# Small tables of eight pair tiles loaded by SyncE, and the last pair's additions split differently

## The chip, the cores and the metric

The kernel runs on one core of a Trainium2 chip. The metric is the device time of one execution in microseconds (us); the median of several executions is compared. The engines are called TensorE (PE, matrix products), VectorE (DVE), ScalarE (ACT), GpSimd (POOL) and SyncE (SP, which here only starts transfers). All of them run at the same time and wait for each other by semaphores.

## What is computed

The first half is a gated linear attention over 4 batches, 8 heads, 768 steps and a head size of 48. Its output, turned into 3072 tokens of 384 values, goes through a router that picks 2 of 8 experts for each token, and then through the experts, each a two-layer network of 384 to 1024 to 384.

```python
for t in range(S):
    state = alpha[:, :, t, :, None] * state + np.einsum('bhd,bhe->bhde', k[:, :, t], v[:, :, t])
    y[:, :, t] = np.einsum('bhd,bhde->bhe', q[:, :, t], state)
...
logits = x @ w_gate
noise_scale = np.log1p(np.exp(x @ w_noise))
noisy_logits = logits + noise_scale * noise
top2 = np.argpartition(-noisy_logits, 2, axis=1)[:, :2]
...
for e in range(E):
    for k in range(2):
        mask = top2[:, k] == e
        h = np.maximum(x[mask] @ w1[e], 0.0)
        out[mask] += top2_w[mask, k, None] * (h @ w2[e])
```

## The kernel before

The attention runs in 24 chunks of 128 tokens. While it does, the router enters each token twice in a table in device memory: one list per expert, each entry four words (token, gate, other expert, rank in the other expert's list). The entries are written by 48 scatters of GpSimd.

The experts then run in 24 *pairs*: a pair is two tiles of 128 tokens of one expert. The pairs 0 to 7 are the first 256 entries of each of the eight experts; the pairs 8 to 23 are two more pairs for each expert, the experts in falling order. Where a pair starts in its list is fixed for the pairs 0 to 13 (`PLANNED`), and for the later ones it is read from a small plan that VectorE computes from the counts. Three smaller tiles (two of 32 tokens, one of 64) take what is left over of the lists; they are worked on beside the pairs 13 to 22. Anything beyond would run under a condition at the end, which isn't met here.

Each pair goes through these steps:

- `load_tab` (lines 1066 to 1076) loads the pair's table, 256 entries of 16 bytes, into a tile `tab` of 128 partitions x 2 x 8. Tiles of that name rotate through six buffers, so that a load waits for the last reader of the table six pairs earlier. It also waits for the scatters that write the entries. SyncE loads it with one transfer for the pairs 0, 1 and 5 to 8; GpSimd loads the others, the pairs 2 to 4 with one transfer and from pair 9 on with two of 128 entries each. From pair 14 on the first row is read from the plan into a register of the engine that loads.
- `load_w1` and `load_w2` (lines 1078 to 1090) load an expert's two matrices on SyncE, where the expert changes. There are two buffers for each.
- `find_rows` on VectorE computes from `tab` which rows to fetch; `gather` on GpSimd fetches the tokens (`x_in`), and `turn_x` transposes them on TensorE.
- 11 products of the first layer and 7 of the second follow, which TensorE sums up in the PSUM banks named a, b, c and A, B, C (`product1`, line 1180, and `product2`, line 1187). The matrices and tokens are added and subtracted beforehand (`sum_w1`, `sum_w2`, `sum_x`), which saves one product in eight in each layer.
- `summed` (line 1199) computes gate x bank + a second term into the tile `o`. `get_prev` (line 921) gathers what the output holds for the pair's tokens into `prev`, and waits for every earlier scatter into the output. `combine` (line 1208) computes previous x second + o, where second is 1 for the second of a token's experts and 0 for the first; `put_pair` scatters the rows to the output (line 929).

The order is written out by hand: each step has a nominal time, pair i is at 20 i, all steps are sorted by that number, and each engine gets its instructions in the sorted order and runs them strictly in it, as soon as their waits are over. `load_tab` is at 20 i - 32, `load_w1` at 20 i - 29.5, `load_w2` at 20 i - 19.8, `find_rows` at 20 i - 27; the first 32-token tile starts loading its table (GpSimd) and its weights (SyncE, by a register that is read from the plan) at 232, the next at 312.

For the last pair, pair 23, `combine` and `put_pair` are replaced by `combine_last` and `put_last`. There the bank C becomes the left half (columns 0 to 191) of the first tile, and the bank A, whose last product ends last, the left half of the second tile.

Of the kernel before, what the change touches and what calls it, by code (L numbers as in the profile page):

```python
# [13 lines left out]
ALU = mybir.AluOpType  # L14
# [4 lines left out]
def kernel(  # L19
# [32 lines left out]
    nc = tc.nc  # L52
    B, H, S, D = q.shape
    N, DM = out.shape
    E, _, F = moe_w1.shape
    C = 128
# [871 lines left out]
    def put_tile(rows, at, beside=()):  # L928
        put = nc.gpsimd.indirect_dma_start(out=out, out_offset=bass.IndirectOffsetOnAxis(ap=at, axis=0), in_=rows,  # L929
                                           in_offset=None, bounds_check=N - 1, oob_is_err=False)  # L930
        for earlier in order["puts"] + order["gets"]:
            tc.declare_no_dep(put.ins, earlier, reason="different rows, or one that this tile has read")
        order["puts"].append(put.ins)
# [6 lines left out]
    def of_plan(i, what, most, engine=mybir.EngineType.SP):  # L940
        return nc.values_load(plan[0:1, i, what:what + 1], engines=[engine], min_val=0, max_val=most,
                              skip_runtime_bounds_check_because=WHY)
# [93 lines left out]
    HF, HD = F // 2, DM // 2  # L1036
# [7 lines left out]
    def pairs(on):  # L1044
# [12 lines left out]
        n_ = block([C, HD], "n", 3)  # L1057
        o = one.tile([C, 2, DM], F32, name="o")
        tabs, wheres, weights, bank = {}, {}, {}, {}
# [5 lines left out]

        def load_tab(i):

            by, engine = (nc.sync, mybir.EngineType.SP) if i < 2 or 5 <= i <= E else (nc.gpsimd, mybir.EngineType.Pool)
            row = order_of[i] * RMAX + [0, R2, 2 * R2][rounds[i]] if i < PLANNED else of_plan(FIRST_PAIR + i - E, 1, TROWS - R2, engine)
            tabs[i] = on["tab"].tile([C, 2, 8], F32, name="tab")  # L1070
            parts = 1 if i <= E else 2
            for s in range(parts):
                take_tile(by.dma_start(out=tabs[i][:, ds(s, 2 // parts), 0:4],
                                       in_=table.bitcast(F32)[ds(row + s * C, R2 // parts), :].rearrange("(s p) w -> p s w", p=C)),
                          2 if i < E else NU)
# [50 lines left out]
        def plus(to, p, q):  # L1126
            nc.vector.tensor_tensor(to, p, q, op=ALU.add)  # L1127
# [65 lines left out]
        gate = lambda i, s: tabs[i][:, s, 1:2]  # L1193

        def scaled(i, to, src, s):
            nc.scalar.activation(to, src, AF.Copy, scale=gate(i, s))  # L1196

        def summed(i, s, d, name, to_add):
            nc.vector.scalar_tensor_tensor(o[:, s, ds(d * HD, HD)], bank[name], gate(i, s), to_add, op0=ALU.mult, op1=ALU.add)

        def get_prev(i):
            for s in range(2):
                get_rows(prev[i % 2][:, s], wheres[i][:, s, 1:2])
# [6 lines left out]
        def combine_last(i):  # L1210

            rows, second = prev[i % 2], tabs[i][:, :, 6:7]
            nc.vector.scalar_tensor_tensor(rows[:, 0], rows[:, 0], second[:, 0], o[:, 0], op0=ALU.mult, op1=ALU.add)
            nc.vector.scalar_tensor_tensor(rows[:, 1, HD:DM], rows[:, 1, HD:DM], second[:, 1], o[:, 1, HD:DM],
                                           op0=ALU.mult, op1=ALU.add)
            nc.vector.tensor_scalar(out=rows[:, 1, 0:HD], in0=rows[:, 1, 0:HD], scalar1=second[:, 1], scalar2=None,
                                    op0=ALU.mult)

        def put_last(i):
            rows = prev[i % 2]  # L1220
            put_tile(rows[:, 0], wheres[i][:, 0, 0:1])
            nc.vector.scalar_tensor_tensor(rows[:, 1, 0:HD], bank["A"], gate(i, 1), rows[:, 1, 0:HD], op0=ALU.mult, op1=ALU.add)
            put_tile(rows[:, 1], wheres[i][:, 1, 0:1])

        def put_pair(i):
            for s in range(2):
# [7 lines left out]
        def steps(i):  # L1234
            w = lambda f, a: w1_(i, f, a)
            v = lambda f, d: w2_(i, f, d)
            late = 11.0 if i >= E and divmod(i - E, 2) in [(g, 0) for g in AFTER_GROUP] else 0.0
            after = 3.5 if i > E and divmod(i - E, 2) in [(g, 1) for g in AFTER_GROUP] else 0.0
            early = {0: EARLY_0, 1: EARLY_1, E: {"find": T * E - 21.5, "gather": T * E - 21.0}}.get(i, {})
            at = lambda name, t: early.get(name, T * i + t) - T * i  # L1240
            return [(T * i + t, go) for t, go in (
                (at("tab", -32.0), lambda: load_tab(i)), (at("w1", -29.5), lambda: load_w1(i)), (at("w2", -19.8), lambda: load_w2(i)),
                (at("find", -27.0), lambda: find_rows(i)), (at("gather", -26.0), lambda: gather(i)),
                (at("turn", -10.1), lambda: turn_x(i)), (at("sum_x", -7.9), lambda: sum_x(i)),
                (at("s0", -16.5), lambda: sum_w1(i, 0)), (at("s1", -15.8), lambda: sum_w1(i, 1)), (at("s3", -7.5), lambda: sum_w1(i, 3)),
                (at("s2", -7.4), lambda: sum_w1(i, 2)),
                (at("t0", -5.2), lambda: sum_w2(i, 0)), (at("t1", -2.5), lambda: sum_w2(i, 1)), (at("t2", 0.1), lambda: sum_w2(i, 2)),
                (at("t3", 4.4), lambda: sum_w2(i, 3)),
                (0.0, lambda: product1("a", w(0, 0), x(0, 0), True)),
                (0.9, lambda: product1("c", w(0, 1), x(1, 0), True)),  # L1250
                (0.95, lambda: nc.scalar.copy(m[0], bank["a"])),
                (1.8, lambda: product1("c", w(0, 2), x(2, 0))),
                (2.7, lambda: product1("b", ws[0], xs[0], True)),
                (2.75, lambda: plus(hs[0][0], bank["c"], m[0])),
                (3.6, lambda: product1("a", ws[1], xs[1])),
                (3.65, lambda: nc.scalar.copy(m[1], bank["b"])),
                (4.5, lambda: product1("b", ws[3], x(1, 1))),
                (4.55, lambda: nc.scalar.copy(m[2], bank["a"])),
                (4.6, lambda: relu(hs[0][0])),
                (5.4, lambda: product1("a", ws[2], xs[2])),  # L1260
                (6.3, lambda: product1("a", w(1, 2), x(2, 1))),
                (7.2, lambda: product1("b", w(0, 2), x(2, 1))),
                (7.25, lambda: plus(hs[1][1], bank["a"], m[1])),
                (8.0, lambda: relu(hs[1][1])),
                (8.1, lambda: product1("a", w(1, 1), xs[3])),
                (8.15, lambda: plus(hs[0][1], bank["b"], m[2])),
                (8.9, lambda: relu(hs[0][1])),
                (9.0, lambda: product1("a", w(1, 2), xs[4])),
                (9.5, lambda: plus(hx[0], hs[0][1], hs[1][1])),
                (9.6, lambda: less(hx[1], hx[0], hs[0][0])),  # L1270
                (9.95, lambda: relu(hs[1][0], bank["a"])),
                (10.0, lambda: less(hx[3], hs[1][0], hx[1])),
                (10.1, lambda: less(hx[2], hs[0][0], hs[0][1])),
                (10.55, lambda: product2("A", hs[0][0], v(0, 0), True)),
                (11.9, lambda: product2("B", hx[0], wt[0], True)),
                (11.95, lambda: scaled(i, n_[0], bank["A"], 0)),
                (13.2, lambda: product2("A", hx[1], wt[1])),
                (13.25, lambda: scaled(i, n_[1], bank["B"], 1)),
                (14.6, lambda: product2("B", hx[3], v(1, 1))),
                (14.65, lambda: scaled(i, n_[2], bank["A"], 0)),  # L1280
                (15.9, lambda: product2("A", hx[2], wt[2])),
                (15.95, lambda: summed(i, 0, 1, "B", n_[2])),
                (17.3, lambda: product2("C", hs[1][0], v(1, 0), True)),
                (17.35, lambda: summed(i, 1, 1, "A", n_[1])),
                (18.6, lambda: product2("A", hs[1][1], wt[3])),
                (18.65, lambda: summed(i, 0, 0, "C", n_[0])),
                (8.5 + late + after, lambda: get_prev(i))) + (((20.0 - 0.05, lambda: scaled(i, o[:, 1, 0:HD], bank["A"], 1)),
                (20.9 + late / 2.4, lambda: combine(i)),
                (22.2 + late / 2.4, lambda: put_pair(i))) if i < NPAIR - 1 else
                ((19.2, lambda: combine_last(i)), (20.0, lambda: put_last(i))))]  # L1290

        return steps, clear_rows, T

# [241 lines left out]
```

## Time and profile before

| | us |
|---|---|
| median of 3 runs | 670.87 |
| lowest and highest run | 669.77, 671.29 |
| the profiled execution, its whole time | 673.52 |
| its span, first to last instruction | 671.9 |
| TensorE busy (matmuls) | 653.7 |
| VectorE busy | 459.2 |
| GpSimd busy | 315.0 |
| ScalarE busy | 270.9 |
| transfers started by GpSimd | 237 |

The profile numbers times from the start of the span. The attention takes the time to about 169, where pair 0 begins. Each pair's first product starts, in us, at 189.1 (pair 1), 209.0, 229.3, 249.4, 269.4, 289.7, 309.8, 329.8 (8), 349.9 (9), 369.8, 389.7, 409.6, 429.5, 451.7, 473.3, 493.2 (16), 513.1, 535.3, 556.8, 576.8, 596.7, 620.4 and 643.2 (23). The busy times and durations come from the one profiled execution.

A line of a timeline has the start, the duration, the engine, the source line, the operation, the tile written `<-` the tiles read, their shapes, and how many such instructions are merged; in brackets, how long the engine had been idle and who released it. The list of waits has the waiting line, who it waited for, and the sum of the waits, their number and the longest. Both can be asked for one engine and one stretch. A second table view gives the busy time of each engine in several stretches.

### The profile page before, as it was taken

The page shows a single profiled execution, that of the slowest core. Times are in us where ns is not written, and L with a number is a line of the kernel's source. Part 1 is how long each engine was busy: PE and PEld are TensorE (multiplying, and loading weights), DVE is VectorE, ACT ScalarE, POOL GpSimd, SP SyncE. Part 2 cuts the span into 40 slices and gives each one's busy share as a digit, 9 for nine tenths or more (in the row PEclk, how much of TensorE's full clock was granted, in tenths as well). Part 3 has the DMA queues.
Part 4 walks back from the last instruction along what each step waited for, and adds up shares of the span by engine and source line. Part 5 has one row for each costly group of instructions (what it writes and reads, how often), then busy time and mean ns, then how long its engine had stood idle before and what let it go on. Part 6 is the DMA issues. An engine that isn't in the chain of part 4 may idle for free. (4 is left out here: it accounts for less than half of the span.)

```text
span 671.9 us, 14849 instructions
## 1 busy us (share of the span) xinstructions
PE 653.7 (97%) x5605; PEld 626.8 (93%) x5605; DVE 459.2 (68%) x1081; ACT 270.9 (40%) x582; POOL 315.0 (47%) x420
## 2 busy tenths in 40 slices
PE   8899999999999999999999999999999999999994
PEld 6898998998999999999999999999999999998894
DVE  6678888885878888767577666575564765647432
ACT  3667667564443434332323332333323333233330
POOL 5362585684344575775514335422654225540231
PEclk9999999999999999999999999999999999999998
DMA  9999988977556657677203476148362483620121
GB/s 140 149 202 173 215 136 155 221 146 218 197 171 231 232 144 231 160 226 255 73 26 129 133 260 215 56 137 293 103 209 67 146 283 113 214 70 8 47 65 37
DMA packets 144181, 105.63 MB, mean 157 GB/s; under 512 B 109255, under 2 KB 131410, under 8 KB 144100
## 3 DMA queue, kind: packets, MB, share of 16 engines
q1 hardware_dynamic: 131716, 80.37, 45.8%
q0 software_dynamic: 12240, 23.80, 11.7%
q8 instruction: 47, 0.77, 0.5%
q10 hardware_dynamic: 144, 0.41, 0.2%
q14 instruction: 34, 0.28, 0.1%
HBM read 94.99 MB, written 14.86 MB: 163 GB/s over the span
## 5 line engine op out<-in xcount | busy, mean ns | idle before, releaser
L936 POOL DMA_INDIRECT x_in<-x_rows,where x48 | 52.5, 1094 | 133.3 <-PE h_ps L1187 60.6
L929 POOL DMA_INDIRECT out_dram<-prev,where x48 | 52.2, 1088 | 60.1 <-DVE prev L1208 37.4
L1180 PE MATMUL sc<-xs,ws 128*128 128x128 f32 x576 | 73.3, 276 | 0.0
L921 POOL DMA_INDIRECT prev<-out_dram,where x48 | 52.3, 1090 | 43.2 <-DMA out_dram<-prev,where 24.5
L1180 PE MATMUL sc<-xt,w 128*128 128x128 f32 x576 | 72.2, 275 | 0.0
L1187 PE MATMUL o_ps<-wt,hx 128*128 128x192 f32 x384 | 70.3, 326 | 0.0
L1191 ACT ACTIVATE h<-h 128x512 f32<-128x512 f32 x72 | 45.5, 631 | 59.6 <-DVE h L1127 59.5
L1180 PEld LDWEIGHTS sc<-xt,w 128*128 128x128 f32 x576 | 69.1, 192 | 0.0
L1180 PEld LDWEIGHTS sc<-xs,ws 128*128 128x128 f32 x576 | 68.3, 192 | 0.4 <-issue 0.2
L1127 DVE TENSOR_TENSOR h<-sc,m 128x512 f32<-128x512 f32 x48 | 33.2, 692 | 44.7 <-PE sc L1180 41.1
L1187 PEld LDWEIGHTS o_ps<-wt,hx 128*128 128x128 f32 x384 | 63.7, 190 | 0.0
L169 POOL DMA_INDIRECT table<-entry,place_u x48 | 55.3, 1153 | 15.7 <-issue 15.0
L396 POOL TENSOR_TENSOR k_P<-k_P,over 128x512 f32<-128x512 f32 (+1 forms) x25 | 28.9, 1157 | 45.2 <-DVE over L378 14.5
L1180 PE MATMUL sc<-xs,w 128*128 128x128 f32 x384 | 49.2, 281 | 0.0
L1196 ACT ACTIVATE o<-o_ps,tab 128x192 f32<-128x192 f32 x23 | 9.6, 419 | 96.1 <-PE o_ps L1187 91.1
L1180 PEld LDWEIGHTS sc<-xs,w 128*128 128x128 f32 x384 | 44.7, 191 | 3.6 <-DVE h L1127 1.7
L1180 PE MATMUL h_ps<-xt,w 128*128 128x128 f32 x384 | 47.1, 276 | 0.0
L338 PE MATMUL tp<-ident,ins 128*128 128x128 f32 x288 | 43.9, 288 | 3.2 <-DMA ins<-in_alpha_dram 2.2
L1180 PEld LDWEIGHTS h_ps<-xt,w 128*128 128x128 f32 x384 | 44.8, 192 | 0.1
L422 DVE COPY_PREDICATED shared<-upto,sc 128x512 f32<-128x512 uint32 x48 | 32.5, 731 | 12.6 <-PE sc L417 12.5
L338 PEld LDWEIGHTS tp<-ident,ins 128*128 128x128 f32 x288 | 33.0, 146 | 8.5 <-ACT ins L356 1.7
L1127 DVE TENSOR_TENSOR h<-h_ps,m 128x512 f32<-128x512 f32 x24 | 16.6, 690 | 34.3 <-PE h_ps L1180 34.2
(257 smaller groups left out, 1435.2 us busy)
## 6 DMA issues: line engine op xcount, KB each, us to landing
w<-in_moe_w_dram SPq DMA_DIRECT2D x30, 1536.0 KB, 8.2
ins<-in_alpha_dram SPq DMA_DIRECT2D x24, 192.0 KB, 5.1
ins<-in_k_dram SPq DMA_DIRECT2D x24, 192.0 KB, 4.9
ins<-in_q_dram SPq DMA_DIRECT2D x24, 192.0 KB, 5.2
vt<-in_v_dram SPq DMA_DIRECT2D x24, 192.0 KB, 4.2
x_rows<-y_sb SPq DMA_DIRECT2D x24, 192.0 KB, 4.5
ins<-in_moe_w_dram SPq DMA_DIRECT2D x3, 1536.0 KB, 12.5
shared<-in_moe_w_dram SPq DMA_DIRECT2D x3, 1536.0 KB, 12.1
```

Source lines behind the costliest of these rows:

```text
L169: put = nc.gpsimd.indirect_dma_start(out=table, out_offset=bass.IndirectOffsetOnAxis(ap=place, axis=0), in_=entry, in_offset=None, bounds_ ...
L338: nc.tensor.transpose(tp[:, j, :], src[:, 2 * j:2 * j + 2, :], ident)
L396: nc.gpsimd.tensor_tensor(c["k"][:, at], c["k"][:, at], over[:, at, 1:CB], op=ALU.mult)
L422: nc.vector.copy_predicated(MTs[n % 2][:, i], mask_upto, sc)
L921: get = nc.gpsimd.indirect_dma_start(out=rows.bitcast(U32), out_offset=None, in_=out.bitcast(U32), in_offset=bass.IndirectOffsetOnAxis(ap= ...
L929: put = nc.gpsimd.indirect_dma_start(out=out, out_offset=bass.IndirectOffsetOnAxis(ap=at, axis=0), in_=rows, in_offset=None, bounds_check= ...
L936: nc.gpsimd.indirect_dma_start(out=rows, out_offset=None, in_=x_rows[0:units * UT, :], in_offset=bass.IndirectOffsetOnAxis(ap=at, axis=0), ...
L1127: nc.vector.tensor_tensor(to, p, q, op=ALU.add)
L1180: nc.tensor.matmul(bank[name][:, f, :], W[:, ds(f * C, C)], X, start=new and f == 0, stop=True, skip_group_check=True)
L1187: nc.tensor.matmul(bank[name], H[:, f, :], W[:, f, :], start=new and f == 0, stop=True, skip_group_check=True)
L1191: nc.scalar.activation(t, t if src is None else src, AF.Relu)
L1196: nc.scalar.activation(to, src, AF.Copy, scale=gate(i, s))
```

## The change

`load_tab`: the pairs 9 to 16 (2 E is 16) are loaded by SyncE instead of GpSimd, each by one transfer instead of two. From pair 14 on, three of them, SyncE reads the first row from the plan. The nominal times stay, so that these loads stand in SyncE's order between the loads of weights; GpSimd starts 221 transfers for 237.

`combine_last` and `put_last`: the last pair's additions are cut into halves of 192 columns. The right halves of both tiles come first. For the left halves, previous x second is prepared ahead (with the term `n_[0]` added for the first tile), and one addition of 192 columns per tile is left that reads the bank C or A. `summed(i, 0, 0, "C", n_[0])` is no longer done for this pair, and the first tile's scatter follows the addition of bank C.

```diff
         def load_tab(i):
-            by, engine = (nc.sync, mybir.EngineType.SP) if i < 2 or 5 <= i <= E else (nc.gpsimd, mybir.EngineType.Pool)
+            by, engine = (nc.sync, mybir.EngineType.SP) if i < 2 or 5 <= i <= 2 * E else (nc.gpsimd, mybir.EngineType.Pool)
             row = order_of[i] * RMAX + [0, R2, 2 * R2][rounds[i]] if i < PLANNED else of_plan(FIRST_PAIR + i - E, 1, TROWS - R2, engine)
             tabs[i] = on["tab"].tile([C, 2, 8], F32, name="tab")
-            parts = 1 if i <= E else 2
+            parts = 1 if i <= 2 * E else 2
             for s in range(parts):
...
         def combine_last(i):
             rows, second = prev[i % 2], tabs[i][:, :, 6:7]
-            nc.vector.scalar_tensor_tensor(rows[:, 0], rows[:, 0], second[:, 0], o[:, 0], op0=ALU.mult, op1=ALU.add)
-            nc.vector.scalar_tensor_tensor(rows[:, 1, HD:DM], rows[:, 1, HD:DM], second[:, 1], o[:, 1, HD:DM],
-                                           op0=ALU.mult, op1=ALU.add)
+            for s in range(2):
+                nc.vector.scalar_tensor_tensor(rows[:, s, HD:DM], rows[:, s, HD:DM], second[:, s], o[:, s, HD:DM],
+                                               op0=ALU.mult, op1=ALU.add)
+            nc.vector.scalar_tensor_tensor(rows[:, 0, 0:HD], rows[:, 0, 0:HD], second[:, 0], n_[0], op0=ALU.mult, op1=ALU.add)
             nc.vector.tensor_scalar(out=rows[:, 1, 0:HD], in0=rows[:, 1, 0:HD], scalar1=second[:, 1], scalar2=None,
                                     op0=ALU.mult)
-        def put_last(i):
+        def put_last(i, s):
             rows = prev[i % 2]
-            put_tile(rows[:, 0], wheres[i][:, 0, 0:1])
-            nc.vector.scalar_tensor_tensor(rows[:, 1, 0:HD], bank["A"], gate(i, 1), rows[:, 1, 0:HD], op0=ALU.mult, op1=ALU.add)
-            put_tile(rows[:, 1], wheres[i][:, 1, 0:1])
+            nc.vector.scalar_tensor_tensor(rows[:, s, 0:HD], bank["CA"[s]], gate(i, s), rows[:, s, 0:HD], op0=ALU.mult, op1=ALU.add)
+            put_tile(rows[:, s], wheres[i][:, s, 0:1])
...
-                (18.65, lambda: summed(i, 0, 0, "C", n_[0])),
-                (8.5 + late + after, lambda: get_prev(i))) + (((20.0 - 0.05, lambda: scaled(i, o[:, 1, 0:HD], bank["A"], 1)),
+                (8.5 + late + after, lambda: get_prev(i))) + (((18.65, lambda: summed(i, 0, 0, "C", n_[0])), (20.0 - 0.05, lambda: scaled(i, o[:, 1, 0:HD], bank["A"], 1)),
                 (20.9 + late / 2.4, lambda: combine(i)),
                 (22.2 + late / 2.4, lambda: put_pair(i))) if i < NPAIR - 1 else
-                ((19.2, lambda: combine_last(i)), (20.0, lambda: put_last(i))))]
+                ((17.9, lambda: combine_last(i)), (18.65, lambda: put_last(i, 0)), (20.0, lambda: put_last(i, 1))))]
```

## The prediction

> **What bounds the kernel now.** I read four views in this order: busy time per engine by stage, who TensorE waits for, TensorE's timeline of one pair of tiles, and then the timelines of GpSimd, SyncE and VectorE around the two places that the change touches.
>
> Busy time by stage (columns: stretch in us, its length, then each engine's busy us and instruction count, granted clock, DMA share, GB/s):
>
> ```profile
> 170.00:350.00 180.00, 180.00 (x1365) 178.00 (x1364) 137.62 (x372) 65.66 (x129) 98.11 (x111) 1.00 0.57 177
> 350.00:470.00 120.00, 120.00 (x926) 116.68 (x925) 78.85 (x191) 41.28 (x83) 45.61 (x48) 1.00 0.51 171
> 470.00:662.00 192.00, 192.00 (x1443) 184.03 (x1442) 107.58 (x262) 62.04 (x124) 73.91 (x77) 1.00 0.36 117
> 662.00:672.00 10.00, 0.66 (x5) 0.36 (x3) 1.45 (x4) 0.00 (x0) 2.02 (x2) 0.70 0.13 43
> ```
>
> TensorE is busy all of the 492 us from 170 to 662; GpSimd (last count) only 45.61 of 120 in the stretch that loses its table loads. The list of waits agrees: over the whole run TensorE waits for gathered rows once (the line below), and asked for the stretch from 170 on, the list is empty, so that once is before 170.
>
> ```profile
> PE x_ps L1118 <- DMA x_in<-x_rows,where: 1.0, 1, 1.0
> ```
>
> Busy matmuls could still be stretched ones, so I look at their spacing (start, us, form). Pair 10:
>
> ```profile
> 369.79 1.05 PE L1180 MATMUL sc<-xt,w 128*128 128x128 f32 x8
> ...
> 379.95 0.82 PE L1118 MATMUL x_ps<-ident,x_in 128*128 128x128 f32 x6
> ...
> 388.41 1.46 PE L1187 MATMUL o_ps<-wt,h 128*128 128x192 f32 x8
> 389.71 0.50 PE L1180 MATMUL sc<-xt,w 128*128 128x128 f32 x3
> ```
>
> One pair takes 389.71 - 369.79 = 19.92 us. Pairs 9, 11 and 12 take 19.91, 19.91 and 19.91 (starts 349.88, 389.71, 409.62, 429.53). Longer pairs have extra matmuls in them (13 and 14 carry a quarter tile: 22.20 and 21.54). A wait on other engines would not repeat to 0.01 us: from pair 0 to the last matmul the limit is TensorE.
>
> So an edit pays only after the last matmul (662.65 by the TensorE timeline), or costs where it makes TensorE wait. That end, on VectorE and GpSimd:
>
> ```profile
> 660.09 0.42 DVE L1199 SCALAR_TENSOR_TENSOR o<-o_ps,tab,n 128x192 f32<-128x192 f32 x1 [0.81 <-PE o_ps L1187]
> ...
> 661.39 0.42 DVE L1199 SCALAR_TENSOR_TENSOR o<-h_ps,tab,n 128x192 f32<-128x192 f32 x1 [0.88 <-PE h_ps L1187]
> 661.85 0.62 DVE L1213 SCALAR_TENSOR_TENSOR prev<-prev,tab,o 128x384 f32<-128x384 f32 x1
> 662.38 0.41 DVE L1214 SCALAR_TENSOR_TENSOR prev<-prev,tab,o 128x192 f32<-128x192 f32 x1
> 662.71 0.32 DVE L1216 TENSOR_SCALAR prev<-prev,tab 128x192 f32<-128x192 f32 x1
> 662.75 1.03 POOL L929 DMA_INDIRECT out_dram<-prev,where  x1 [8.20 <-DVE prev L1213]
> 663.14 0.42 DVE L1222 SCALAR_TENSOR_TENSOR prev<-o_ps,tab,prev 128x192 f32<-128x192 f32 x1
> 664.08 0.98 POOL L929 DMA_INDIRECT out_dram<-prev,where  x1 [0.31 <-issue]
> ```
>
> VectorE ends at 663.56, but the second scatter starts at 664.08, not some 0.28 us later as the first did after its release (661.85 + 0.62 = 662.47 to 662.75): it stands behind the first on GpSimd (662.75 + 1.03 + 0.31 = 664.09). So the first scatter sets the end, not the last addition.
>
> **What the Trainium skill says.** "DMA: Bandwidth & Descriptors", section "Issuing engines are not separate DMA queues": transfers begun on different engines run on the same 16 DMA engines, and spreading them saves only the sequencer time of starting them. So I expect GpSimd time from the moved tables and no bandwidth; no row of this trace shows more. The same page, "Where the ~2 µs actually goes", puts most of a small transfer's fixed 2 us into the write receipt: this trace has 2.76 us for a scatter from start to landing (the piece at 647.68 of the chain of waits), and nothing edited shortens that. "Perfetto Trace Analysis", section "Tensor Engine Instruction (MATMUL, LD_WEIGHTS)": the end of a matmul is estimated, not observed; hence the check by spacing above.
>
> **The change part by part.**
>
> *Tables off GpSimd.* Pairs 9 to 16 took two issues each on GpSimd, 16 in all. The line of table loads shows 33 at a median of 597 ns, two together 1.17 us:
>
> ```profile
> 373.33 1.17 POOL L1073 DMA_DIRECT2D tab<-table  x2
> ```
>
> 16 x 0.585 = 9.4 us leave GpSimd between 315 and 480, with the register loads of pairs 14 to 16. Behind each couple stand the two gathers of previous rows, up to 1.17 us earlier now where they did not wait for a scatter to land. Beyond them is only VectorE's combination, which no matmul reads. TensorE's gathers have no wait to lose. Worth at the end: 0.
>
> *Tables onto SyncE.* Eight issues at 0.37 to 0.58 us (rows at 305.42, 248.81, 268.66; one took 1.51). Each is one transfer of 256 rows. By the built order, two (9, 10) come ahead of pair 10's weights, two (11, 12) ahead of 12's, one (13) behind those, one (14) behind the first quarter tile's weights and ahead of pair 14's, two (15, 16) ahead of 16's. SyncE runs in order, so a table that waits holds the weights behind it:
>
> ```profile
> 305.42 0.37 SPq L1073 DMA_DIRECT2D tab<-table  x1
> 305.89 0.55 SPq L946 DMA_DIRECT2D w<-in_moe_w_dram  x1
> ...
> 360.23 0.37 SPq L946 DMA_DIRECT2D w<-in_moe_w_dram  x1
> ...
> 400.05 0.38 SPq L946 DMA_DIRECT2D w<-in_moe_w_dram  x1
> ...
> 440.37 0.37 SPq L946 DMA_DIRECT2D w<-in_moe_w_dram  x1
> ```
>
> What can a table wait for? First, its buffer: six rotate, so table i waits for pair i-6's last use (table 12: the combination at 311.05 to 312.2). Second, the plan, for 14 to 16, which the quarter tile's weights on this queue await already, until 389.12. Third, list entries: table 8 ends that wait at 305.42. Pair 10's weights go about 2 x 0.45 = 0.9 us later. Those of 12, 14 and 16 wait for their own buffer until 360.23, 400.05 and 440.37, after the tables ahead are through: 0. With 8.2 us to land (page, part 6), the first halves for 12, 14 and 16 arrive at 368.4, 408.3 and 448.6; VectorE first reads them at 393.48, 433.79 and 477.04. Slack is 25.1, 25.5 and 28.4 us. The tables come early too: number 14 goes out near 390.5 and, even behind 12.1 us of weights, lands by 403; its first reader is at 424.1. Cost: 0, with at least 25 us of cover.
>
> *The last pair's additions.* Removed: one 384-wide addition (619 ns) and the sum of bank C into o. Added: a 192-wide addition and a last one of 192 from bank C. New VectorE order from the row at 660.09: two additions of right halves, one with n, one multiplication, then C, then A. Spacing: 661.39 to 661.85 is 0.46 after a sum out of PSUM, 662.38 to 662.71 is 0.33 after a 192-wide one. So they start at 660.55, 660.88, 661.21, 661.54, and C at 661.87 (up to 661.97 if it waits a full write, as the 0.11 ahead of 663.14 suggests). C's bank is ready at 661.39. C ends at 662.29 to 662.39 and the first scatter starts 0.28 later, at 662.57 to 662.67, instead of 662.75. A starts when its bank is done, about 662.69, and ends 663.11 instead of 663.56; the second scatter still follows the first: 663.91 to 664.01 instead of 664.08. Gain on this chain: 0.07 to 0.17 us. The branch of the last engine leaves with VectorE's end, 0.45 us earlier, so 0.45 is the upper bound if that is what the tail of 671.9 - 665.06 = 6.8 us follows. Below nothing: previous rows are now read 1.3 us earlier (660.55 for 661.85), but their second gather was issued by 654.55 and lands near 657.3 at 2.76 us; no loss. I take 0.2 us.
>
> *Sum.* 0 + 0 - 0.2. On the profiled execution's own 673.52 us (span 671.9 and 1.62 around it) that is 673.3. That execution stands 2.65 above the median of the runs, and the edit is the same in both: 670.87 - 0.2 = 670.7.
>
> **Rivals.**
>
> *GpSimd's relief reaches the end.* If each couple of table loads were in a chain that TensorE follows, up to 8 x 1.17 = 9.4 us would go: 661.5. For it: gathers of previous rows wait 24.5 us in all for scatters, so GpSimd is not slack everywhere. Against it: TensorE waits for none of it from 170 on, and pairs 9 to 12 are equal to 0.01 us.
>
> *The tail shortens by more.* GpSimd's sequencer shows nothing between 666.9 and 668.3 in the tail, 1.4 us whose reason I can't read. If starting earlier removes it as well: 670.87 - 0.2 - 1.4 = 669.3. For: the tail is all latency. Against: landing and closing barrier are unchanged.
>
> *Slower: a table holds the weights on SyncE.* Place: the table of pair 14, ahead of the weights for 14. It decides from 433.79 - 8.2 = 425.6 on: each us held past that is a us of TensorE. A buffer or plan that came free at 429.5, when pair 13 starts, would cost 4 us: 674.8. For: the queue is in order and three tables read the plan there. Against: every condition I can name is met by 391.
>
> **How the numbers follow.** No change is what a measurement can't tell from none, 0.2% or 1.34 us: the three runs span 1.52. Forecast as worked: 0.70. Relief 0.08, shorter tail 0.10, slower 0.12 with unnamed costs of the moved order. Of the forecast's 0.70, scatter about a gain of 0.2 puts 0.07 below 669.53 and little above 672.2, and rivals of small size leave 0.01 within 0.2%. So faster 0.25, within 0.2% 0.64, slower 0.11. The likeliest time is 670.7; its own range is 669.6 to 671.6. Taking in the shorter tail and the first part of the slower case, 669.0 to 671.8.
>
> **What would show it.** In the changed profile: 17 table issues on GpSimd for 33 and 14 on SyncE for 6; TensorE's starts of pairs 9 to 16 unmoved to within 0.1 us, and no wait from 170 on; weights for 12, 14 and 16 still 20 us or more ahead of their readers; one addition after the last matmul, from about 662.7; the first scatter near 662.6 and the second right behind it. I am wrong if a pair between 9 and 16 changes its 19.91 us, if SyncE shows a table waiting beyond 400, or if the time between the last scatter and the end differs from 6.8 us.

## The result and the profile after

The changed kernel takes 680.82 us (median of 6 runs, 678.64 to 682.92), the kernel before 671.28 us (6 runs, 669.77 to 675.93). The ratio is 1.0129, 95% interval 1.0098 to 1.0159: slower by 9.5 us. Medians are over all runs; ratios and their intervals, here and below, leave out runs over 1.5% above the fastest of their kernel.

TensorE lost nothing. Its busy time by stage, of the kernel after (stretch in us, its length, then busy us and instruction count of TensorE, its weight load, VectorE, ScalarE and GpSimd, clock, DMA share, GB/s):

```profile
170.00:350.00 180.00, 180.00 (x1365) 178.01 (x1364) 137.51 (x372) 65.67 (x129) 96.21 (x107) 1.00 0.57 178
350.00:470.00 120.00, 120.00 (x926) 116.69 (x925) 78.82 (x191) 41.27 (x83) 38.52 (x36) 1.00 0.50 171
470.00:662.00 192.00, 192.00 (x1443) 184.03 (x1442) 108.39 (x263) 62.04 (x124) 74.25 (x77) 1.00 0.36 117
662.00:680.00 18.00, 0.53 (x4) 0.23 (x2) 0.42 (x1) 0.00 (x0) 2.02 (x2) 0.60 0.07 24
```

In the second line GpSimd's count falls from 48 to 36 and its busy time from 45.61 to 38.52; TensorE is as full as before. Its timeline around pair 10, after (start, us, form):

```profile
349.77 1.05 PE L1180 MATMUL sc<-xt,w 128*128 128x128 f32 x8
...
369.68 1.05 PE L1180 MATMUL sc<-xt,w 128*128 128x128 f32 x8
...
389.58 1.05 PE L1180 MATMUL sc<-xt,w 128*128 128x128 f32 x8
```

19.91 and 19.90 us a pair, each start 0.11 to 0.13 us earlier than before, and so to the end. SyncE's own timeline, after, has the moved tables ahead of the weights:

```profile
305.41 1.47 SPq L1073 DMA_DIRECT2D tab<-table  x3
307.00 0.40 SPq L946 DMA_DIRECT2D w<-in_moe_w_dram  x1
308.39 0.37 SPq L948 DMA_DIRECT2D w<-in_moe_w_dram  x1
308.85 3.94 SPq L1073 DMA_DIRECT2D tab<-table  x2
360.11 0.37 SPq L946 DMA_DIRECT2D w<-in_moe_w_dram  x1
...
399.93 0.38 SPq L946 DMA_DIRECT2D w<-in_moe_w_dram  x1
```

The weights of pair 10 go 1.1 us later (307.00 for 305.89), those of 12 and 14 with TensorE's 0.12 us earlier. The last part of the work, after, all engines:

```profile
659.97 0.42 DVE L1199 SCALAR_TENSOR_TENSOR o<-o_ps,tab,n 128x192 f32<-128x192 f32 x1 [0.81 <-PE o_ps L1187]
660.30 0.74 DVE L1214 SCALAR_TENSOR_TENSOR prev<-prev,tab,o 128x192 f32<-128x192 f32 x2
...
660.96 0.41 DVE L1216 SCALAR_TENSOR_TENSOR prev<-prev,tab,n 128x192 f32<-128x192 f32 x1
661.07 1.46 PE L1187 MATMUL o_ps<-wt,h 128*128 128x192 f32 x8
661.29 0.31 DVE L1217 TENSOR_SCALAR prev<-prev,tab 128x192 f32<-128x192 f32 x1
661.52 0.41 DVE L1222 SCALAR_TENSOR_TENSOR prev<-h_ps,tab,prev 128x192 f32<-128x192 f32 x1
662.21 1.03 POOL L929 DMA_INDIRECT out_dram<-prev,where  x1 [7.79 <-DVE prev L1222]
662.57 0.42 DVE L1222 SCALAR_TENSOR_TENSOR prev<-o_ps,tab,prev 128x192 f32<-128x192 f32 x1 [0.64 <-PE o_ps L1187]
663.54 0.99 POOL L929 DMA_INDIRECT out_dram<-prev,where  x1 [0.31 <-issue]
```

The last scatter starts at 663.54 instead of 664.08. The last work is begun 0.54 us earlier, yet the span ends at 679.7 instead of 671.9. The page shows no busy time in between, since semaphore instructions and the like aren't counted as busy. They are found by asking for the lines of the program's end (line, queue, operation, count, then min/median/max ns, first to last start). The kernel before:

```profile
L1495 POOLq INC_SWDGE_SEM  x1: 612/612/612, 668.6 to 668.6; - x1
L1530 POOLq DRAIN  x3: 46/103/1786, 669.2 to 671.6; - x3
```

The kernel after:

```profile
L1494 POOLq INC_SWDGE_SEM  x1: 2532/2532/2532, 666.7 to 666.7; - x1
L1529 POOLq DRAIN  x3: 46/103/9632, 669.3 to 679.4; - x3
```

GpSimd's closing, a semaphore instruction of its software DMA queue and then a drain (the longest of three is the one that matters), takes 2.53 + 9.63 = 12.16 us instead of 0.61 + 1.79 = 2.40. What the two do inside is not in the trace. The closing begins 1.9 us earlier (666.7 for 668.6): the last scatter starts 0.54 us earlier, and by its landing signals in the trace it has landed 2.79 us after its start instead of 4.17. So 9.76 - 1.9 = 7.9 us, which is what the span grew by (679.7 - 671.9 = 7.8).

The quicker landing isn't the change's doing: over the fifteen profiles of this document that scatter took 2.79 to 4.73 us, 4.44 in e1 and 4.64 in e2 below, which have half of the change each. The medians grew by 9.5 and not 7.8 us because the execution profiled before was 2.2 us above its median (673.52, 671.28), the one after 0.5 (681.31, 680.82).

### The profile page after: what moved, and what is told of

Same layout as the page of the kernel before. It is cut to its first block, busy times and chain, and to the rows that moved or that the text cites. A ratio compares the mean times of both kernels' runs of the same rounds, so it can differ in the third digit from the quotient of the medians.

```text
span 679.7 us, 14840 instructions
## 1 busy us (share of the span) xinstructions
PE 655.0 (96%) x5605; PEld 627.8 (92%) x5605; DVE 458.7 (67%) x1082; ACT 270.7 (40%) x582; POOL 306.3 (45%) x404
```

## The experiments

The question is what makes the closing long: the tables (fewer transfers, fewer rows, another program) or the earlier last scatters.

### One part of the change at a time

Tables alone (label e1_tables_only): the edit of `load_tab` on the kernel before.

> The table loads of pairs 9 to 16 moved to SyncE as in the change, the last pair's additions as before. In the changed kernel the last matmul ends as early as before and the 9 us lie in GpSimd's closing drain (9.63 us for 1.79). Theory 'count': that drain depends on how many transfers GpSimd began in the execution; then this one (221) shows the long drain, span about 680, some 9 us above before. Theory 'end': the earlier last scatters make the drain long; then this one is within 1 us of before, with a drain near 1.8.

Measured 680.76 us, ratio 1.0143 (1.0126 to 1.0160). Its closing:

```profile
L1495 POOLq INC_SWDGE_SEM  x1: 2532/2532/2532, 666.2 to 666.2; - x1
L1530 POOLq DRAIN  x3: 46/103/9632, 668.7 to 678.9; - x3
```

To the nanosecond the closing of the changed kernel. The additions alone (e2_additions_only):

```diff
-if i < 2 or 5 <= i <= 2 * E else
+if i < 2 or 5 <= i <= E else
-            parts = 1 if i <= 2 * E else 2
+            parts = 1 if i <= E else 2
```

> Only the last pair's additions split as in the change, the tables as before (237 transfers of GpSimd). Theory 'count': drain near 1.8 us, time 0.3 to 0.6 us below before (the last addition of VectorE started 0.57 us earlier in the changed kernel). Theory 'end': drain near 9.6 us, some 9 us above before.

Measured 670.94 us, ratio 0.9989 (0.9980 to 0.9997), closing 0.612 and 1.786 us. So theory "end" falls: the whole loss is in the tables, and the split additions gain 0.11%, or 0.7 us, by the ratio; the medians differ by 0.3 us only.

One transfer of GpSimd for each table instead of two (e3_one_transfer), on the kernel before:

```diff
-            parts = 1 if i <= E else 2
+            parts = 1 if i <= 2 * E else 2
```

> As before, but the tables of pairs 9 to 16 loaded by GpSimd with one transfer of 256 entries each instead of two of 128: 229 transfers of GpSimd, the same bytes and rows. Theory 'count': a drain between or unlike both, so a time that differs from before by up to 9 us, although nothing on the way to the last matmul changes. Theory 'end': as before, within 1 us.

Measured 671.16 us, ratio 0.9993 (0.9969 to 1.0016), closing 0.612 and 1.786 us: eight transfers fewer with the same rows change nothing.

Spare transfers put the number back (e4_spare_transfers), on the changed kernel:

```diff
             parts = 1 if i <= 2 * E else 2
+            if E < i <= 2 * E:
+                for s in range(2):
+                    nc.gpsimd.dma_start(out=spare[:, s], in_=moe_noise[ds(s * C, C), 0:4])
```

> The changed kernel with two spare transfers of GpSimd (128 rows of 16 bytes into a tile that nobody reads) beside each of the eight moved table loads: 237 transfers again, the rest as in the changed kernel. It does work that the result does not need. Theory 'count': drain near 1.8 us again, time 0.3 to 0.6 us below before. Theory 'end': drain near 9.6 us, some 9 us above before.

Measured 671.28 us, ratio 1.0007 (0.9993 to 1.0021). Its closing:

```profile
L1498 POOLq INC_SWDGE_SEM  x1: 612/612/612, 666.2 to 666.2; - x1
L1533 POOLq DRAIN  x3: 46/103/1786, 666.9 to 669.2; - x3
```

More work on GpSimd, all of it useless, brings the 9 us back: the tables on SyncE are not slow, their absence on GpSimd is. The additions are split here too, but their gain doesn't show. Whether transfers or rows count, and by what law, is open: e3 changed the transfers alone, and by half as many.

### Transfers, rows or the program's length

Eight spare transfers of few rows (e5_few_rows), on the changed kernel:

```diff
+            if E < i <= 2 * E:
+                nc.gpsimd.dma_start(out=spare, in_=moe_noise[ds(i * C, 16), 0:4])
```

> The changed kernel with one spare transfer of GpSimd of only 16 rows of 16 bytes beside each of the eight moved table loads: 229 transfers in all, but hardly more rows (128 of the 2048 that moved to SyncE). It loads data that nobody reads. Theory 'transfers' (the closing drain depends on the number of transfers GpSimd began; 229 was short with one transfer per table): drain 1.79 us, time about 671. Theory 'rows' (it depends on how many rows[...] GpSimd wrote): drain 9.63 us, time about 680. Theory 'program' (it depends on the length of GpSimd's program): undecided between them.

Measured 681.18 us, ratio 1.0135 (1.0096 to 1.0174). Its closing is neither of the two expected, and even longer:

```profile
L1497 POOLq INC_SWDGE_SEM  x1: 2652/2652/2652, 665.9 to 665.9; - x1
L1532 POOLq DRAIN  x3: 46/103/10122, 668.6 to 679.3; - x3
```

One spare transfer of many rows (e6_many_rows), on the changed kernel:

```diff
+            if i == E + 1:
+                nc.gpsimd.dma_start(out=spare, in_=moe_noise[ds(0, 16 * C), 0:4].rearrange("(s p) e -> p s e", p=C))
```

> The changed kernel with a single spare transfer of GpSimd of 2048 rows of 16 bytes, beside the table load of pair 9: 222 transfers, as many rows as before the change. It loads data that nobody reads. Theory 'transfers': drain 9.63 us, time about 680, unless the limit lies just at 222. Theory 'rows': drain 1.79 us, time about 671. Theory 'program' (one instruction more than the changed kernel): drain 9.63 us.

Measured 671.54 us, ratio 1.0011 (0.9996 to 1.0027). Its closing:

```profile
L1497 POOLq INC_SWDGE_SEM  x1: 852/852/852, 666.0 to 666.0; - x1
L1532 POOLq DRAIN  x3: 46/103/2766, 666.9 to 670.2; - x3
```

229 transfers can close long (e5) and 222 short (e6), so their number alone doesn't decide; rows fit better. The packets that the page counts for GpSimd's queue (q0) don't decide either: 11984 in e3, which closes short, and in e5. Rows and bytes are not told apart, since every row here has 16 bytes. And 2.77 us is not 1.79: there aren't just two values.

Fills instead of transfers (e7_fills), on the changed kernel:

```diff
+            if E < i <= 2 * E:
+                for s in range(4):
+                    nc.gpsimd.memset(spare[:, s], 0.0)
```

> The changed kernel with 32 small fills on GpSimd (128 x 4 values that nobody reads), four beside each moved table load: GpSimd's program is as long as before the change or longer, but it begins 221 transfers. Theories 'transfers' and 'rows': drain 9.63 us, time about 680. Theory 'program': drain 1.79 us, time about 671.

Measured 680.70 us, ratio 1.0128 (1.0089 to 1.0167), closing 2.532 and 9.632 us: 32 more instructions of GpSimd change nothing.

More transfers than before (e8_more_transfers): the sixteen spare ones of e4 added to the kernel before.

> The kernel before with 16 spare transfers of GpSimd of 128 rows each: 253 transfers and 2048 rows more than before. It loads data that nobody reads. If the drain is long below a limit and short above it (theories 'transfers' or 'rows' with a threshold): drain 1.79 us, time as before. If it follows a place in a ring that comes round: another value is possible, 9.63 us among them. TensorE's end must not move, since GpSimd has room.

Measured 672.90 us, ratio 1.0035 (1.0018 to 1.0052): slower. Its closing:

```profile
L1499 POOLq INC_SWDGE_SEM  x1: 932/932/932, 665.9 to 665.9; - x1
L1534 POOLq DRAIN  x3: 46/103/3092, 666.9 to 670.5; - x3
```

A threshold with a short side falls: above the rows of before the closing grows again, by 0.32 and 1.31 us for 2048 rows. New theory: GpSimd's transfers are entered in a ring, a buffer that is filled in a circle; the closing grows with the rows since the ring last came round, and is small just after.

### The closing foretold and measured

The edit is the changed kernel with another last pair on SyncE (12, 20, 10, and later 14, for 2 E) in both lines of `load_tab`:

```diff
-if i < 2 or 5 <= i <= 2 * E else
+if i < 2 or 5 <= i <= 12 else
-            parts = 1 if i <= 2 * E else 2
+            parts = 1 if i <= 12 else 2
```

> The change with the tables of pairs 9 to 12 alone on SyncE (those of 13 to 16 on GpSimd as before) and the additions split: 229 transfers of GpSimd, 1024 rows fewer than before. So far 2048 rows more than before made the semaphore instruction 0.32 us and the closing drain 1.31 us longer (0.61 to 0.93, 1.79 to 3.09), and 2048 rows fewer made them 1.92 and 7.85 us longer. Theory 'place in a ring' (both grow with the rows since the ring last came round): half of a step down, semaphore instruction 0.45 us, drain 1.13 us, time about 1.3 below before with the 0.5 of the additions, near 669.8; or, if the ring comes round between these counts, 2.69 and 10.28 us and a time near 680. Theory 'two levels' (short at or above some number of rows, long below): 0.61 and 1.79, or 2.53 and 9.63, nothing between.

> The change carried on: the tables of pairs 9 to 20 on SyncE and the additions split, 213 transfers of GpSimd, 1024 rows fewer than in the changed kernel. Theory 'place in a ring': shorter than in the changed kernel by half a step, semaphore instruction 2.37 us (2.53 - 0.16), drain 8.98 us (9.63 - 0.65), time about 0.8 below the changed kernel. Theory 'two levels': 2.53 and 9.63 us again. A theory by which fewer transfers of GpSimd always close later expects more than 9.63.

> The change with the tables of pairs 9 and 10 alone on SyncE and the additions split: 233 transfers of GpSimd, 512 rows fewer than before. Theory 'place in a ring': a quarter of a step down, semaphore instruction 0.53 us, drain 1.46 us, time about 0.9 below before with the additions, near 670.2; or, if the ring comes round before that, 2.77 and 10.61 us and a time near 680. Theory 'two levels': 0.61 and 1.79 us, or 2.53 and 9.63.

The closing of e9_tables_to_12:

```profile
L1494 POOLq INC_SWDGE_SEM  x1: 432/432/432, 682.5 to 682.5; - x1
L1529 POOLq DRAIN  x3: 46/103/1051, 683.0 to 684.6; - x3
```

The closing of e10_tables_to_20:

```profile
L1494 POOLq INC_SWDGE_SEM  x1: 2372/2372/2372, 689.2 to 689.2; - x1
L1529 POOLq DRAIN  x3: 46/103/8978, 691.6 to 701.1; - x3
```

e11 has 0.512 and 1.377. Foretold were 0.45 and 1.13 for e9, 2.37 and 8.98 for e10, 0.53 and 1.46 for e11: met for e10, and missed by 0.02 and 0.08 us for the other two. Theory "two levels" falls. The times of this group say little: the kernel before took 692.81 us in it (681.74 to 701.80). The ratios were 0.9993 (0.9957 to 1.0029) for e9, 1.0110 (1.0023 to 1.0197) for e10 and 1.0018 (0.9980 to 1.0056) for e11.

The kernel of e9 was timed once more:

> The kernel with the tables of pairs 9 to 12 on SyncE and the additions split once more, timed apart from the earlier run, in which the kernel before took 692.8 us itself. Its closing is known from that run: semaphore instruction 0.43 us (0.18 below before), drain 1.05 us (0.74 below before); VectorE's last addition and the last scatter start 0.5 us earlier. Theory 'place in a ring': the same 0.43 and 1.05 us again, and 0.9 to 1.4 us below before, a ratio of 0.9979 to 0.9987. Were the closing not part of the time, the ratio would be 0.9993 or above.

The closing was 0.432 and 1.051 again. The ratio, 1.0038 (1.0007 to 1.0069), is outside what was expected, and on the side expected if the closing were no part of the time. It comes from a group in which the kernel before took 694.14 us (682.78 to 700.63), and the medians, 693.12 for 694.14, stand the other way round. In that profile TensorE waits between 170 and 350 (busy 164.13 us of 180), as in those of e9, e10 and e11 (170.27, 164.61, 164.22), which neither kernel did in the first result. I don't know where that comes from. A gain of 1 us is not shown: that the closing is part of the time rests on the runs in which it changed by over 9 us (e1, e5 and e7 against e4 and e6).

> The change with the tables of pairs 9 to 14 on SyncE and the additions split: 225 transfers of GpSimd, 1536 rows fewer than before. With 1024 rows fewer the closing was short (0.43 and 1.05 us), with 2048 fewer long (2.53 and 9.63). Theory 'place in a ring': either not yet come round, semaphore instruction 0.35 us, drain 0.73 us, time some 1.7 us below before (ratio 0.997 to 0.998), or come round already, 2.61 and 9.95 us, time about 9 us above before. Theory 'two levels' or a drain that follows the count of transfers: a value between, such as 5 us.

The closing of e13_tables_to_14:

```profile
L1494 POOLq INC_SWDGE_SEM  x1: 352/352/352, 674.9 to 674.9; - x1
L1529 POOLq DRAIN  x3: 46/103/724, 675.3 to 677.0; - x3
```

Measured 677.38 us, ratio 0.9988 (0.9962 to 1.0015), the kernel before at 678.00. It has not come round. All runs but e5 and e6, sorted by the rows that GpSimd moves:

| rows against before | runs | semaphore instruction, us | drain, us |
|---|---|---|---|
| +2048 | e8 | 0.932 | 3.092 |
| 0 | before, e2, e3, e4 | 0.612 | 1.786 |
| -512 | e11 | 0.512 | 1.377 |
| -1024 | e9, e12 | 0.432 | 1.051 |
| -1536 | e13 | 0.352 | 0.724 |
| -2048 | after, e1, e7 | 2.532 | 9.632 |
| -3072 | e10 | 2.372 | 8.978 |

On both sides of the jump 1024 rows are worth 0.16 and 0.65 us (0.512 - 0.352, 2.532 - 2.372; 1.377 - 0.724, 9.632 - 8.978). Carried on from -1536, the row -2048 would be 0.272 and 0.397; it is 2.26 and 9.235 us above. At these slopes the jump is 14,464 rows by the one and 14,477 by the other (2.26 x 1024 / 0.16; 9.235 x 1024 / 0.6532). All the differences in the table are, to within 0.01 us, whole steps of 0.020 us in the semaphore instruction and 0.0817 us in the drain, a step for each 128 rows (with one exception, below); the jump is 113 steps in both. So the two instructions follow one count, and that count starts afresh somewhere between -1536 and -2048 rows. A ring would do that. That it comes round every 14,464 rows is an estimate: the runs cover 5120 rows and one jump.

The ring itself isn't in the trace. The Trainium skill has the pieces: "DMA: Bandwidth & Descriptors", section "SWDGE vs HWDGE vs iDMA", says that GpSimd appends the descriptors of its transfers to rings, and "Runtime: NRT & Kernel Launch", section "The ~15µs preamble/postamble breakdown", has a reset of the DMA rings with a barrier at the end, at about 2 us. If the drain is that reset, which no run tells, then 2 us is no constant here: 0.72 to 10.12 us were measured.

Rows alone are not its exact measure. From -512 to 0 the closing grows by five steps (0.100 and 0.409 us), where four would be due. Eight transfers of 16 rows (e5) added 0.12 and 0.49 us, as much as 768 rows, six times their own; one of 2048 rows (e6) stands 0.24 and 0.98 us above sixteen of 128, as if it had 1536 more. How a transfer is counted stays open.

## Why the prediction was wrong

- "From pair 0 to the last matmul the limit is TensorE": right. No wait from 170 on, pairs at 19.90 to 19.91 us.
- "Tables onto SyncE", cost 0: right. Table 14 goes out at 391.28 (said: near 390.5), the weights of 12 and 14 at 360.11 and 399.93. The slack was never called on.
- "Tables off GpSimd. Worth at the end: 0": this step failed. It counted what the 16 transfers cost while they were issued (9.4 us, hidden) and let what they leave behind for GpSimd's closing be nothing. That was the missing term: -2048 rows took the closing over its jump, +1.92 us for the semaphore instruction and +7.85 us for the drain. e1 and e4 show it from both sides. The passage on issuing engines that the prediction cites holds for the transfers (DMA share 0.50 for 0.51 between 350 and 470); of the program's end it doesn't speak.
- "The tail of 671.9 - 665.06 = 6.8 us" was carried over as a constant, and the second rival leaned on "landing and closing barrier are unchanged". I had seen that tail as latency after the last scatter; 2.40 us of it were GpSimd's closing, and the lines of the program's end had that in plain view. In the changed kernel the tail is 679.7 - 664.53 = 15.2 us. The prediction named this as a sign of being wrong. The 1.4 us in the tail that it couldn't read are the last scatter's landing: fifteen of its sixteen landing signals had come by 666.9, the last at 668.25. The 2.76 us that it took for a scatter were too short for this one.
- "The last pair's additions", 0.07 to 0.17 us by the scatters, 0.2 taken: right in its mechanism, too small. Seen from the last matmul (0.12 us earlier in this profile), the last scatter gained 664.08 - 663.54 - 0.12 = 0.42 us. The spacing was mis-sized: the first prepared addition started 0.33 us after the sum ahead of it (660.30 - 659.97), not 0.46, since it begins before that sum is over, and the addition of bank C started 0.23 us after the multiplication (661.52 - 661.29), not 0.33. e2 has 0.7 us for the part by itself (0.2 to 1.3 by its interval).
- The slower rival had the wrong place, weights held on SyncE. The right one, a cost after the last work, was not among the rivals.

Of the change, the additions may be worth keeping: e2 beats the kernel before by 0.11%, with an interval that ends just short of none. With them, tables up to pair 14 on SyncE shorten the closing by 1.32 us more (0.352 + 0.724 for 0.612 + 1.786), but the time of e13 has an interval that takes in no change. Two pairs more, 15 and 16, take the closing from 1.08 to 12.16 us.

## What to carry to other kernels

Read the stretch after the last work line by line, sequencer instructions too, before taking it for a constant: an edit that touches no critical path can still change it. Where GpSimd issues many transfers, time the closing drain after each change in their number or size, since less work there can cost more, and useless work can pay. A profile's chain of waits ends at the last instruction that did something; compare its end with the span (664.5 and 679.7 us in the changed kernel).

## What was not expected of the hardware

GpSimd's closing took the same times to the nanosecond wherever the rows were the same and came in transfers of 128 or 256: 2.532 and 9.632 us in three kernels, 0.612 and 1.786 in four, 0.432 and 1.051 in e9 and e12, whose spans were 684.9 and 698.5 us. That speaks for work that is counted out, not for a wait. It ranged from 1.08 us (e13) to 12.77 us (e5), with nothing in the busy times to tell of it. Beside that, the tables that SyncE starts right behind weights took long to land: in the changed kernel 6.6 us (369.03), 10.5 (391.28) and 7.3 (410.3), where those with no weights just ahead took 1.7 to 3.0. The change didn't bring this about, since a table that was not moved has it too (9.8 us, 248.7); the trace of the kernel before has landing times for tables of the quick kind alone.
